# Sliding-window attention and a gated convolution network: casts on two engines, copies for the shifted gate blocks, fillers on TensorE, and a target for each task

## The chip, the cores and the metric

The kernel runs on one core of one Trainium2 chip. The metric is the device time of one execution in microseconds. Five engines share the work: TensorE (PE, with weight loads shown apart as PEld), VectorE (DVE), ScalarE (ACT), GpSimd (POOL) and SyncE (SP), whose queue issues nearly all DMAs.

## The reference, cut to what matters

```python
# q, k, v: 8 batches x 8 heads x 576 rows x 64 columns, float32
scores = q @ k.T / sqrt(64)                 # only |row - column| <= 32 counts
attn = softmax(scores) @ v                  # per head; heads side by side: x is 8 x 576 x 512
h = maximum(x @ w_in, 0)                    # 512 -> 1024
conv = sum over kk of conv_w[kk] * h shifted by kk - 1 along the rows   # 3 taps per channel
out = (h * sigmoid(conv)) @ w_out           # 1024 -> 512, float32
```

## The kernel before

**Attention.** A batch has eight heads, worked on in four pairs. q, k and v come from DRAM in float32 into staging tiles (`qkst`, `vst`) and are cast to bf16 (`qkb`, `ve`). `ve` holds v in blocks of 128 rows with a column of ones; `vo` is the same shifted by 64 rows, made by two copies of 64 partitions. `transposes` turns q and k on PE (18 small products each) and copies them out of PSUM into `qT` and `kT`. `scores` makes nine bands of 128 x 64 for a pair, takes the exponential on ACT (two calls, 640 and 512 elements) and multiplies by a band mask on DVE (`attn<-attn,mask`, 1152 elements). `values` multiplies by v (the ones give the sum), takes the reciprocal and scales into `xn`. `x_turned` turns `xn` on PE and copies it to `xT`.

**The network.** The rows of two batches (1152) are cut into three chunks of 384, so there are twelve chunks, c = 0 to 11; chunk 1 is done in two halves. `first` multiplies by w_in in eight blocks m of 128 channels (four products each) and writes half of the rectified result to `hT`. `gates` does the three taps as 48 small products of 32 x 32 weights per group of four blocks (`hT,diag_w`), takes tanh on ACT (two calls per group) into `tn`, and makes three products on DVE (`gT<-tn,hT` and `gT<-tn,gT`), which give twice h times the sigmoid. The small products put channel block m on partitions turned by 32 times (m mod 4). So for three blocks of four, h has to stand in `gT` in the same turned order: `moves` does that with DMAs from `hT` to `gT` on SP's queue. The w_out rows are loaded turned in the same way. `second` multiplies `gT` by w_out, 128 rows at a time, eight products each, copies the result to `wst` and stores it. PSUM is one tile of eight banks; a task that opens banks gets them when their readers are done. `ws` (`wst`) is also the staging of w_in and w_out.

**What sets the order.** Nothing runs in the order in which it is written. Each step is a task, put in by `Order.add` with the engines it may run on and a modelled time for each, the data it reads and writes, the banks it opens, and a target time t. `Order.run` is a list scheduler that plays all engines forward in modelled time: an engine takes the ready task with the smallest target; a task with a choice of ACT or DVE goes where it ends first. The instructions are emitted in the order found, and each engine keeps that order on the chip. The targets follow from some thirty numbers in `PARAMS`: when a pair of heads or a chunk starts and how far each kind of step lies from that. All casts are tasks of POOL alone. Most instructions are issued through one helper line, line 274, so the profile's rows are told apart by tile and shape.

The functions that the change and the prediction touch are `Order.add`, `Order.run`, `loads`, `load_w_in`, `load_w_out`, `transposes`, `scores`, `values`, `x_turned`, `first`, `moves`, `gates`, `second` and `ffn`.

Of the kernel before, what the change touches and what calls it, by code (L numbers as in the profile page):

```python
# [14 lines left out]
RING = 3100  # L15

# [15 lines left out]
class Order:  # L32
# [3 lines left out]
    def __init__(self):  # L36
        self.tasks, self.writer, self.readers = [], {}, {}

    def add(self, kinds, emit, t, reads=(), writes=(), opens=None, ps=(), after=(), claims=()):


        deps = set(after)
# [10 lines left out]
        task = Task(len(self.tasks), kinds, emit, t, deps, opens, ps)  # L53
        task.soft = soft - deps
        for k in reads:
            self.readers.setdefault(k, []).append(task)
# [8 lines left out]
    def run(self, emit=True):  # L65
        free = {"PE": 0.0, "ACT": 2800.0, "DVE": 6000.0, "POOL": 4400.0, "SP": 800.0}
        mode, channel, backlog = None, 0.0, []
        bank_free = [0.0] * 8
        for x in self.tasks:
# [39 lines left out]
        while pending:  # L109
            best = None  # L110
            for e, xs in ready.items():
# [5 lines left out]
                while pick is None:  # L117
# [28 lines left out]
            if len(x.kinds) > 1:  # L146
                def done(k):
                    return max(free[k], x.ready) + x.kinds[k][1]
                f = min(x.kinds, key=done)
                if f != e:  # L150
                    e, now = f, max(free[f], x.ready)
                    busy, result, more = x.kinds[e]
            if e == "PE":
                if more != mode:
                    busy, result, mode = busy + 90.0, result + 90.0, more
            if e == "SP":
# [8 lines left out]
                result = channel + slack - now  # L165
            free[e] = now + busy
# [28 lines left out]
def kernel(  # L195
# [53 lines left out]
    hT_pp = [sb([128, MB, CH + (4 if i == 1 else 2)], BF16, f"hT{i}") for i in range(3)]  # L249
# [14 lines left out]
    mask = sb([128, 2, S], BF16, "mask")  # L264

# [24 lines left out]
    def pl(n):  # L290
        return 150 + 0.85 * n, 200 + 0.85 * n, None
# [12 lines left out]
    o = Order()  # L304
    nc.scalar.dma_start(conv_w24, moe_conv_w.rearrange("k (m p) -> (k m) p", p=128))
# [32 lines left out]


# [8 lines left out]

    def loads(b):
        i = b % NLD  # L350

        def load_qk(y, j):
# [4 lines left out]
            )  # L357

# [21 lines left out]
        if b < 2:  # L380
            x, dx = (-100.0 if b == 0 else -50.0), 0.1
# [5 lines left out]
        def paced():  # L387
            return before[-2:-1] if b > 1 and len(before) > 1 else []

        for j in range(NPH):  # L390
            for y in range(2):
                t = x + n * dx
                o.add({"SP": dma(256, 110)}, lambda e, y=y, j=j: load_qk(y, j), t,
                      writes=[("st", y, j)], after=paced())
                before.append(o.tasks[-1])
                o.add({"POOL": pl(1152)}, lambda e, y=y, j=j: cast_qk(y, j, e), t,
                      reads=[("st", y, j)], writes=[("b", i, y, j)])
                n += 1
        for c in range(NBLK):
            t = x + n * dx  # L400
            o.add({"SP": dma(1024, 21)}, lambda e, c=c: load_v(c), t, writes=[("vst", c)], after=paced())
            before.append(o.tasks[-1])
            o.add({"POOL": pl(512)}, lambda e, c=c: cast_v(c, e), t,
                  reads=[("vst", c)], writes=[("ve", i, c)])
            n += 1
        for cs in ((0, 2), (2, 4)) if b == 0 else ((0, 4),):
            for half in range(2):
                o.add({"DVE": dve(520 * (cs[1] - cs[0]), 4)},
                      lambda e, cs=cs, half=half: shift(half, cs), x + n * dx,
                      reads=[("ve", i, c + half) for c in range(*cs)],  # L410
                      writes=[("vo", i, c, half) for c in range(*cs)])

    def load_w_in():
        for h in range(2):
# [9 lines left out]
            o.add({"SP": dma(512, 95)}, load, -60.0, writes=[("ws", 4 * h + c) for c in range(4)])  # L424
            for c in range(KC):
                o.add({"POOL": pl(512)}, lambda e, h=h, c=c: cast(e, h, c), -60.0 + h,
                      reads=[("ws", 4 * h + c)], writes=[("w_in", h, c)])

    def load_w_out():
        rows = moe_w_out.rearrange("(h c p) f -> p h c f", c=4, p=128)  # L430
        for c in range(4):
            def load(e, c=c):
                for lo, at, n in turn(c):
# [5 lines left out]
            o.add({"SP": dma(256, 95, len(turn(c)))}, load, -40.0,  # L439
                  writes=[("ws", 4 * h + c) for h in range(2)])  # L440
            for h in range(2):
                o.add({"POOL": pl(512)}, lambda e, h=h, c=c: copy(e, w_out_sb[:, 4 * h + c, :], ws[:, 4 * h + c, :]),
# [18 lines left out]
    def conv_weights():  # L461
        ps = Banks(1)
        o.add({"PE": pe(200.0, "f32")},
              lambda e: tensor.matmul(bank(ps, 0)[:, 0:3 * MB], conv_w24, ident24, start=True, stop=True),
              5.0, opens=ps, writes=[("cw24",)])
        o.add({"DVE": dve(24)}, lambda e: vector.tensor_copy(
            out=conv_w_sb.rearrange("p k m -> p (k m)"), in_=bank(ps, 0)[:, 0:3 * MB]),
            5.0, reads=[("cw24",)], writes=[("cw",)], ps=[ps])
        o.add({"DVE": dve(768)}, lambda e: vector.tensor_tensor(
# [5 lines left out]
    def transposes(g2):  # L475
# [3 lines left out]
        i, n = b % NLD, g2 % NKT  # L479
        for y in range(2):  # L480
# [16 lines left out]
            o.add({"PE": pe(280.0, "rows")}, mm, t + Q["TR"],  # L497
                  reads=[("b", i, y, j)], writes=[("tr", g2, y)], opens=ps,
                  claims=[("T", n, y, h) for h in range(2)])
            for h in range(2):  # L500
                o.add({"ACT": act(576), "DVE": dve(576)},
                      lambda e, ps=ps, h=h, to=to: copy(
                          e, to[:, h, :, :], half(ps, h).rearrange("p (j x) -> p x j", x=64)),
                      t + Q["TC"], reads=[("tr", g2, y)], writes=[("T", n, y, h)], ps=[ps])
# [4 lines left out]
    def scores(g):  # L509
# [3 lines left out]
        for part, ts in enumerate((range(0, 5), range(5, 9))):  # L513
            ps = Banks(2, 2)
            w = 64 * len(ts)

# [10 lines left out]
            o.add({"PE": pe(28.0 * len(ts), "rows")}, mm, t + Q["SC"] * d,  # L527
# [340 lines left out]
```

## Time and profile before

| what | value |
|---|---|
| median of 3 runs (lowest, highest) | 241.9 us (240.6, 242.52) |
| the profiled execution's own time | 243.37 us |
| its span | 241.7 us |
| PE busy | 208.1 us (86%) |
| ACT busy | 164.0 us (68%) |
| DVE busy | 160.1 us (66%) |
| POOL busy | 80.9 us (33%) |
| read from and written to DRAM | 32.52 MB, 9.44 MB |

An engine's busy time counts the stretches in which at least one of its instructions runs. A group's mean is the length of one instruction, which can overlap the next by a little. "L274" is the helper line. A row of the order of time gives start, length, engine, operation, tiles and count, and in brackets how long the engine was idle before it and what ended that wait. A tile's row gives the shortest, median and longest length. PEclk is the share of the full TensorE clock that was granted.

### The profile page before, as it was taken

To read this page: it belongs to the slowest core of one execution; us is meant where nothing else is said; L and a number is where in the kernel's file an instruction comes from. 1 tells how busy PE (TensorE), PEld (TensorE's weight loads), DVE (VectorE), ACT (ScalarE), POOL (GpSimd) and SP (SyncE) were. 2 spreads that over 40 slices of the span, in tenths; PEclk is the share of its full clock that TensorE was granted. 3 is DMA by queue.
4 is the path that set the end of the run, shared out by engine and by line. 5 is a ranking of instruction groups with operands and counts; after the bars stand their busy time and mean duration, and the time that the engine had idled before them with its cause. 6 is when DMAs were issued, how large, how long until landed. Compare 5 with 4: busy or idle time off the path is not lost. (4 is left out here: it accounts for less than half of the span.)

```text
span 241.7 us, 9128 instructions
## 1 busy us (share of the span) xinstructions
PE 208.1 (86%) x3878; PEld 124.3 (51%) x3906; DVE 160.1 (66%) x268; ACT 164.0 (68%) x291; POOL 80.9 (33%) x96
## 2 busy tenths in 40 slices
PE   1536995589998869999999998999999999999993
PEld 0425464365655454565455654655555655555541
DVE  7586166998575899546399779698684595524140
ACT  1650586445698576679977886679778885876751
POOL 5757744536613444662236517321000000000000
PEclk9999999758999997999999999999999999999999
DMA  6999999989698899969489989756132223342534
GB/s 237 292 289 392 248 233 223 275 229 337 168 290 186 217 293 355 328 186 278 98 207 356 264 225 281 161 129 205 37 129 55 79 105 68 123 110 54 177 113 181
DMA packets 67228, 49.62 MB, mean 205 GB/s; under 512 B 46172, under 2 KB 52340, under 8 KB 67188
## 3 DMA queue, kind: packets, MB, share of 16 engines
q1 hardware_dynamic: 67152, 49.03, 71.6%
q8 instruction: 30, 0.49, 0.9%
q14 instruction: 10, 0.08, 0.1%
q10 hardware_dynamic: 36, 0.01, 0.0%
HBM read 32.52 MB, written 9.44 MB: 174 GB/s over the span
## 5 line engine op out<-in xcount | busy, mean ns | idle before, releaser
L274 PE MATMUL pst<-xT,w_in_sb 128*128 128x385 bf16 (+2 forms) x416 | 75.4, 322 | 1.6 <-ACT xT L274 0.6
L274 PE MATMUL pst<-w_out_sb,gT 128*128 128x512 bf16 x260 | 64.3, 384 | 3.2 <-issue 2.2
L274 PEld LDWEIGHTS <-w_in_sb 128*128 128x128 bf16 x416 | 37.6, 100 | 25.8 <-issue 3.4
L274 ACT ACTIVATE hT<-pst 128x385 bf16<-128x385 f32 (+2 forms) x80 | 38.6, 489 | 11.1 <-PE pst L274 10.1
L274 DVE SCALAR_TENSOR_TENSOR gT<-tn,gT 128x384 bf16<-128x384 f32 (+2 forms) x52 | 42.4, 842 | 3.9 <-DMA gT<-hT 3.9
L274 POOL CAST ve<-vst 128x512 bf16<-128x512 f32 x40 | 29.4, 741 | 45.7 <-DMA vst<-in_v_dram 43.5
L274 ACT ACTIVATE attn<-pst 128x640 bf16<-128x640 f32 x64 | 39.4, 667 | 4.9 <-PE pst L274 4.9
L274 PEld LDWEIGHTS <-gT 128*128 128x128 bf16 x288 | 26.6, 99 | 31.0 <-issue 3.3
L274 ACT ACTIVATE tn<-pst 128x768 f32<-128x768 f32 (+1 forms) x52 | 37.4, 768 | 6.5 <-PE pst L274 4.6
L274 ACT COPY wst<-pst 128x512 f32<-128x512 f32 x36 | 21.2, 588 | 29.6 <-PE pst L274 28.1
L274 DVE TENSOR_TENSOR attn<-attn,mask 128x1152 bf16<-128x1152 bf16 x32 | 26.9, 846 | 12.3 <-ACT attn L274 12.1
L274 DVE TENSOR_TENSOR xn<-pst,rec 128x640 bf16<-128x640 f32 x32 | 25.8, 818 | 0.5
L274 DVE SCALAR_TENSOR_TENSOR gT<-tn,hT 128x384 bf16<-128x384 f32 (+1 forms) x26 | 14.7, 564 | 16.5 <-ACT tn L274 16.4
L274 POOL CAST qb<-qst 128x1152 bf16<-128x1152 f32 x16 | 19.9, 1242 | 16.2 <-DMA qst<-in_q_dram 12.5
L274 POOL CAST kb<-kst 128x1152 bf16<-128x1152 f32 x16 | 19.9, 1243 | 16.0 <-DMA kst<-in_k_dram 14.3
L274 PE MATMUL pst<-hT,diag_w 32*32 32x384 bf16 (+1 forms) x1248 | 21.2, 322 | 1.8 <-DVE xn L274 1.0
L274 ACT COPY xT<-pst 128x1024 bf16<-128x1024 bf16 (+1 forms) x16 | 11.8, 781 | 13.9 <-PE pst L274 13.9
L274 PEld LDWEIGHTS <-attn 128*64 128x64 bf16 x640 | 14.1, 119 | 13.6 <-issue 8.6
L274 PE MATMUL pst<-ve,attn 128*64 128x65 bf16 x384 | 17.4, 206 | 3.8 <-DVE attn L274 2.3
L274 PE MATMUL pst<-qT,kT 64*128 64x64 bf16 x576 | 17.5, 197 | 3.1 <-DVE kT L274 0.8
L274 PE MATMUL pst<-vo,attn 128*64 128x65 bf16 x256 | 15.6, 206 | 3.3 <-DVE vo L274 3.3
L274 PEld LDWEIGHTS <-kT 64*128 64x128 bf16 x576 | 12.2, 98 | 12.0 <-issue 9.2
(37 smaller groups left out, 163.4 us busy)
## 6 DMA issues: line engine op xcount, KB each, us to landing
qst<-in_q_dram SPq DMA_DIRECT2D x16, 576.0 KB, 6.4
kst<-in_k_dram SPq DMA_DIRECT2D x16, 576.0 KB, 7.3
out_dram<-wst SPq DMA_DIRECT2D x11, 768.0 KB, 5.8
vst<-in_v_dram SPq DMA_DIRECT2D x24, 256.0 KB, 5.5
vst<-in_v_dram SPq DMA_DIRECT2D x16, 192.0 KB, 5.9
wst<-in_moe_w_in_dram SPq DMA_DIRECT2D x2, 1024.0 KB, 7.9
gT<-hT SPq DMA_DIRECT2D x14, 144.0 KB, 3.6
gT<-hT SPq DMA_DIRECT2D x34, 48.0 KB, 2.1
```

The costliest lines, as they stand in the source:

```text
L274: return lambda *args, **kwargs: fixed(do(*args, **kwargs))
```

## The change

1. **Casts on ACT or POOL.** Every cast of q, k, v, w_in and w_out may now run on either, wherever it is planned to end first.
2. **A port in the plan.** The scheduler has one more resource, `port`. POOL's tasks and DVE's tasks with two inputs in SBUF (and the copies between SBUF tiles) may not overlap in planned time. Nothing on the chip enforces it.
3. **Copies in place of moves.** For all twelve chunks `moves` now issues copies from `hT` to `gT`, 32 or 64 partitions at a time, on DVE or ACT. `hT` gets one leading column. The DMA form remains in the text for c >= `GE`, and there are only twelve chunks.
4. **Fillers.** Where the plan shows PE idle, before 95 us, it gets products of a constant tile, 128 x 512, written to a bank that PE's next task opens and overwrites: 28 of them.
5. **A target for each task.** The list `TIMES` gives a target for every task of a kind, in the order in which they are added, instead of the formula. `PARAMS` changes too.
6. **Batch 0 in halves.** q and k of batch 0 are loaded, cast and turned in two halves of 32 partitions; some k loads go through ACT's queue. Scores, masks and values of batch 0 come in two parts, and the first product of chunk 0 too. w_in's halves are loaded behind the halves of batch 0.
7. **Smaller things.** The table for the exponential is loaded by a small call at the start; the rule that a load waits for the second load before it is off.

The program orders show this count: POOL had all 88 casts; after the change there are 92 (batch 0's are halves), 53 on POOL and 39 on ACT. DVE gets 121 copies and ACT 49 for the moves. SP issues 102 DMAs fewer for the moves.

The core of the diff:

```diff
+        t = next(self.times[name], t) if name in self.times else t
...
+                if pick and pick[1].kinds[e][2] == "port":
+                    pick = (max(pick[0], port), pick[1], pick[2])
...
+            if more == "port":
+                port = now + busy
...
+            if e == "PE" and emit and now < KEEP:
+                since = max(free[e], bank_free[where[0]], 4000.0)
+                self.warm(int((now - since - 300.0) / (260.0 if free[e] > 4000.0 else 430.0)), where[0])
...
-    hT_pp = [sb([128, MB, CH + (4 if i == 1 else 2)], BF16, f"hT{i}") for i in range(3)]
+    hT_pp = [sb([128, MB, CH + (6 if i == 1 else 4)], BF16, f"hT{i}")[:, :, 1:] for i in range(3)]
...
+    def warm(n, i):
+        for _ in range(n):
+            tensor.matmul(pst[:, i, :], warm_sb[:, 0:128], warm_sb, start=True, stop=True)
...
-            return before[-2:-1] if b > 1 and len(before) > 1 else []
+            return before[-2:-1] if b > 1 and len(before) > 1 and not GE else []
...
-                o.add({"POOL": pl(1152)}, lambda e, y=y, j=j: cast_qk(y, j, e), t,
+                o.add("qc", {"POOL": pl(1152), "ACT": act(1152)}, lambda e, y=y, j=j: cast_qk(y, j, e), t,
...
             ms = [4 * qd + s_ for qd in qds]
+            wide = 64 if s_ == 2 else 32
+            for lo in range(0, 128, wide) if c < GE else ():
+                to = (lo + 32 * s_) % 128
+                def shift(e, m=ms[0], lo=lo, to=to, wide=wide):
+                    if len(qds) > 1:
+                        copy(e, gate(m, to, to + wide, 2, 4), taps(m, 1, lo, lo + wide, 2))
+                    else:
+                        copy(e, gate(m, to, to + wide), taps(m, 1, lo, lo + wide))
+                o.add("mc", {"DVE": two(dve(n * len(qds) + 60, 3.4)), "ACT": act(n * len(qds))},
+                      shift, t + Q["MC"], reads=[("h", kind, m, p_) for m in ms for p_ in halves],
...
-            o.add({"DVE": dve(n * count)}, product, late,
+            o.add("pr", {"DVE": two(dve(n * count))}, product, late,
...
+        if c == 0:
+            for m in range(MB):
+                first(c, m, 0, T0 + Q["A0"] + m * 0.5)
```

More of the change, by code (lines that the diff above doesn't have):

```diff
@@ L15 @@
 RING = 3100
+KEEP = 95000.0
+GE = 12
 class Banks:
@@ L53, in add @@
         task = Task(len(self.tasks), kinds, emit, t, deps, opens, ps)
+        if line:
+            soft.add(line[-1])
+        if line is not None:
+            line.append(task)
         task.soft = soft - deps
+        task.tag = (name, index)
         for k in reads:
@@ L357, in load_qk, with load_half, cast_half @@
             )
+        def load_half(y, j, half):
+            for e_ in range(2):
+                src = (q, k)[y][b, 4 * j + 2 * e_:4 * j + 2 * e_ + 2, 32 * RP * half:32 * RP * half + 32 * RP, :]
+                (scalar if y and not half else sync).dma_start(
+                    qkst[y][j][64 * e_:64 * e_ + 64, half, :, :].rearrange("p j d -> p (j d)"),
+                    bass.AP(src.tensor, src.offset, [[RP * D, 32], [S * D, 2], [1, RP * D]]),
+                )
+        def cast_half(y, j, half, e):
+            copy(e, half_of(y, j, half), qkst[y][j][:, half, :, :])
         def cast_qk(y, j, e):
@@ L437, in load @@
                     )
[L439 to L440 removed]
+            o.add("wo", {"SP": dma(256, 95, len(turn(c)))}, load, -90.0,
+                  writes=[("ws", 4 * h + c) for h in range(2)], line=lead)
             for h in range(2):
[L442 removed]
+                o.add("woc", {"POOL": pl(512), "ACT": act(512)}, lambda e, h=h, c=c: copy(e, w_out_sb[:, 4 * h + c, :], ws[:, 4 * h + c, :]),
                       T1 - 2 + h, reads=[("ws", 4 * h + c)], writes=[("w_out", 4 * h + c)])
@@ L479, in transposes @@
         i, n = b % NLD, g2 % NKT
+        if b == 0:
+            for half in range(2):
+                for y in range(2):
+                    transposes_half(g2, y, half, t + Q["B0"] * half)
+            return
         for y in range(2):
@@ L820 @@
             scores(2 * g2 + 1)
-        for i in range(NP):
-            values(b * NP + i)
+        for part in (0, 1) if b == 0 else (None,):
+            for i in range(NP):
+                values(b * NP + i, part)
         for c, n in ((0, 2), (2, 2), (4, 1)):
```

267 lines of the change are left out of this document (183 added, 84 removed), and 114 rows, old and new, of tables (PARAMS, TIMES).

## Prediction

> **What bounds the kernel now.** I read the busy time of each engine by stretches first, cut where a stage of the work ends: 42 is where the last of chunk 0's tanh calls ends, 70 chunk 1's, 122 chunk 4's, 174 chunk 7's.
>
> ```profile
> core 0: us, PE busy (x) PEld busy (x) DVE busy (x) ACT busy (x) POOL busy (x), PEclk, DMA share, GB/s
> 0.00:42.00 42.00, 24.66 (x514) 17.75 (x514) 25.51 (x57) 20.52 (x35) 25.62 (x38) 1.00 1.01 274
> 42.00:70.00 28.00, 23.63 (x528) 15.69 (x530) 23.13 (x39) 16.63 (x34) 14.69 (x15) 0.82 0.87 258
> 70.00:122.00 52.00, 47.44 (x914) 27.85 (x917) 36.21 (x56) 40.68 (x72) 21.40 (x24) 0.97 0.87 240
> 122.00:174.00 52.00, 49.72 (x965) 28.72 (x973) 42.48 (x65) 39.86 (x73) 19.16 (x20) 1.00 0.78 216
> 174.00:221.00 47.00, 46.00 (x801) 26.28 (x805) 27.85 (x48) 36.33 (x66) 0.00 (x0) 1.00 0.30 90
> ```
>
> From 122 on PE is the bound (95.7 of 99 us busy). Before it, PE is short of work: it misses 17.3, 4.4 and 4.6 us in the first three stretches, and DMA is busy 0.87 to 1.01 there. So the start is bound by loads, casts and the chain of small attention steps, the rest by PE. Next, the order of time around the first uses of both weights, and the end:
>
> ```profile
> 25.54 4.12 PE L274 MATMUL pst<-xT,w_in_sb 128*128 128x385 bf16 x16 [0.55 <-ACT xT L274]
> 42.11 3.27 POOL L274 CAST w_out_sb<-wst 128x512 bf16<-128x512 f32 x4 [1.39 <-DMA wst<-in_moe_w_out_dram]
> 54.62 2.37 PE L274 MATMUL pst<-w_out_sb,gT 128*128 128x512 bf16 x7
> ...
> 120.51 1.51 ACT L274 ACTIVATE tn<-pst 128x768 f32<-128x768 f32 x2 [0.15 <-PE pst L274]
> ...
> 231.13 6.85 PE L274 MATMUL pst<-w_out_sb,gT 128*128 128x512 bf16 x31 [0.16 <-issue]
> 238.07 0.59 ACT L274 COPY wst<-pst 128x512 f32<-128x512 f32 x1 [1.20 <-PE pst L274]
> ```
>
> The first product with w_in starts at 25.5, the first with w_out at 54.6, twelve microseconds after the last w_out block landed (42.1). The chip then works through PE's queue until 238.0; the last store adds 3.7 to the span's 241.7. The profiled execution took 243.4, its span 241.7; the median of the three runs is 241.9, so I make the sum on the span and add 0.2.
>
> **The change part by part.** The program order of each engine gives the counts; every stretch below is cut at the same event, chunk 4's last tanh (the 24th on ACT; 122.0 before).
>
> *Copies in place of moves.* All 102 issues of shifted gate blocks leave SP's queue and the DMA; 170 copies come, 121 on DVE, 49 on ACT.
>
> ```profile
> L274 SPq DMA_DIRECT2D gT<-hT x102: 496/627/1922, 34.6 to 230.2; - x102
> ...
> L274 DVE COPY vo<-ve x18: 425/698/1587, 13.8 to 167.2; 64x2080 bf16<-64x2080 bf16 x14, 64x1040 bf16<-64x1040 bf16 x4
> ```
> ```profile
> L274 ACT COPY wst<-pst 128x512 f32<-128x512 f32 x36 | 21.2, 588 | 29.6 <-PE pst L274 28.1 <-issue 1.0 <-POOL ve L274 0.5
> L274 ACT COPY xT<-pst 128x1024 bf16<-128x1024 bf16 x10 | 10.1, 1017 | 13.7 <-PE pst L274 13.7
> L274 ACT COPY qT<-pst 128x576 bf16<-128x576 bf16 x23 | 14.2, 647 | 0.3 <-PE pst L274 0.3
> L274 DVE COPY xT<-pst 128x1024 bf16<-128x1024 bf16 x6 | 4.1, 691 | 7.8 <-PE pst L274 7.7
> L274 DVE COPY kT<-pst 128x576 bf16<-128x576 bf16 x13 | 9.7, 750 | 3.0 <-PE pst L274 2.9
> ```
>
> The nearest DVE row is the vo copy, also bf16 from SBUF to SBUF across partitions: 0.425 us for 1040 elements and 0.70 for 2080 undisturbed, so 0.15 + 0.000264 per element: 0.35 us for 768, 0.25 for 384. The other end is the kT row, one element at a time out of PSUM (0.750 for 576): 0.95 and 0.55. I take the fast end because hT gets a leading column in the same change, which puts the middle tap on an even element as vo's is. ACT: the line through 588 (512) and 1017 (1024) gives 0.80 and 0.48. Up to chunk 4 the cost is 21 x 0.35 + 29 x 0.25 = 14.7 us of DVE and 9 x 0.80 + 11 x 0.48 = 12.5 us of ACT. SP gains 102 x about 0.63 us of issue, in which its loads and stores stood behind it. The later loads also lose their pacing (each waited for the second one before it), so they start once their staging is free; I cost that at nothing, hidden from 122 on by PE's own work, and its failure is the loads rival below.
>
> *Casts.* 39 of 92 now stand on ACT, 53 on POOL (88 before); up to chunk 4 ACT gets: 10 of 1152 elements (1.13 by the line), 22 of 512 (0.59), 3 of 576 (0.65), 26.2 us. Against it, ten copies of xT and wst go from ACT to DVE (-9.0), and half-size pieces of batch 0 and chunk 0 add 5.7. ACT: 12.5 + 26.2 - 9.0 + 5.7 = +35.4 us in whole lengths; DVE: 14.7 + 7.6 of moved xT and wst copies + 10.3 of pieces = +32.6. Lengths overlap in a queue: before, ACT's own instructions up to there add up to 84.4 by such lengths where the first three stretches show 77.8 busy, DVE's 90.7 against 84.9. So after the change ACT has 110.5 us of busy time by that event and DVE 115. If all follow without a gap, less: two tanh calls take 1.51 where the group's mean is 0.819 each, 0.13 less per instruction, which makes ACT's 196 instructions 102 us.
>
> *The start.* Batch 0 comes in halves and chunk 0's first product is cut in two, so half of it no longer waits for the whole batch. ACT begins at 5.4 instead of waiting for the first copies, but has 2 us of gaps until the loads are in. Both engines then carry what PE waits for. So chunk 4's last tanh falls between 5.4 + 102 = 107.4 and 5.4 + 110.5 + 2 = 117.9 without any other waits; I take the middle of 102 and 110.5, with the 2 us: 113.6 instead of 122.0.
>
> *Fillers.* 28 products of 512 columns, 0.22 each by the last PE row above (6.85 / 31): 6.2 us. They lie in gaps that the planned times show, and cost nothing while the next task waits for ACT or DVE longer than they last; if no gap is there, 6.2. What they can bring:
>
> ```profile
> 45.00:55.00 10.00, 7.22 (x173) 5.20 (x168) 9.14 (x17) 3.67 (x6) 3.82 (x4) 0.52 0.88 279
> 55.00:60.00 5.00, 4.89 (x59) 2.81 (x60) 4.76 (x7) 2.72 (x7) 2.92 (x4) 0.94 1.10 329
> 89.00:93.00 4.00, 3.52 (x41) 2.58 (x42) 3.94 (x4) 3.07 (x5) 2.59 (x3) 0.59 1.08 363
> ```
> ```profile
> 46.14 0.26 PE L274 MATMUL pst<-ve,attn 128*64 128x65 bf16 x1 [1.00 <-DVE attn L274]
> 47.83 0.26 PE L274 MATMUL pst<-ve,attn 128*64 128x65 bf16 x1 [0.93 <-DVE attn L274]
> 49.78 1.67 PE L274 MATMUL pst<-ident,xn 128*128 128x128 bf16 x14 [0.85 <-DVE xn L274]
> ```
>
> The clock stood at 0.52 in 45 to 55 and 0.59 in 89 to 93, with PE busy 7.22 and 3.52: at full clock that is 3.4 and 1.4 us less. I count none of it by itself, since both stretches lie ahead of chunk 4, where ACT and DVE now set the pace. The page "TensorE: Matmul & The Clock Gate" of the Trainium skill (section "Why this matters for your kernels") speaks against fillers here: the clock falls only when PE idles for more than about 3 us between bursts. By that page fillers in gaps of 1 us would bring nothing, only their 6.2 us could count, and the sum would be 236; the rows show the half clock with gaps of 0.85 to 1.00, so the measurement differs, and the sum stays as it is.
>
> *After chunk 4.* By that event the new order has 12 w_in products, 36 transposes, 36 scores and 40 value products more behind it:
>
> ```profile
> 222.48 2.13 PE L274 MATMUL pst<-xT,w_in_sb 128*128 128x385 bf16 x12
> 57.26 0.44 PE L274 MATMUL pst<-ident,qb 64*128 64x64 bf16 x18
> 57.53 0.43 PE L274 MATMUL pst<-ident,kb 64*128 64x64 bf16 x18
> 42.03 0.44 PE L274 MATMUL pst<-qT,kT 64*128 64x64 bf16 x18
> 42.39 0.22 PE L274 MATMUL pst<-ve,attn 128*64 128x65 bf16 x1
> ```
>
> That is 12 x 0.17 + 2 x 0.27 + 2 x 0.36 (start to start) + about 0.7 for the values = 4.0 us. PE needed 238.0 - 122.0 = 116.0 from there; it now needs 112.0, if no wait is added. DVE is what comes late next: between chunks 4 and 7 it gets 32 copies (15 x 0.35 + 17 x 0.25 = 9.5 us) on top of 42.5 in 52 us, which just fits.
>
> **Sum:** 113.6 + 112.0 + 3.7 = 229.3, and 0.2 for the median: 229.5, said as 230. Ends: 107.4 and no PE idling after chunk 4 (3.3 us less than before) give 219.8 with the 3.7; 117.9 gives 233.8.
>
> **The rivals.**
> *The copies are slow (slower).* If a copy runs at the kT row's rate, DVE gets 21 x 0.60 + 29 x 0.30 = 21 us more before chunk 4, that event falls at 134.6 and the time is 251 or more (134.6 + 112.0 + 3.7 + 0.2). It decides from 126.0 on (126.0 + 115.9 = 241.9), 12 us more of DVE. For it: the copies change partitions within the tile and the tap view has two levels. Against it: vo changes partitions too.
> *DVE and POOL hold each other up.* The targets keep two-input DVE tasks away from POOL's by planned times only; nothing enforces it.
>
> ```profile
> L274 DVE TENSOR_TENSOR attn<-attn,mask x32: 695/758/1561, 11.4 to 198.7; 128x1152 bf16<-128x1152 bf16 x32
> ...
> L274 DVE TENSOR_TENSOR attn<-attn,mask 128x1152 bf16<-128x1152 bf16 x32 | 26.9, 846 | 12.3 <-ACT attn L274 12.1
> ```
>
> The mask product takes 695 undisturbed and 846 on average: 0.15 us each. Masks, vo copies, gate products and now gate copies are 124 such tasks by chunk 4 instead of 66; at 0.15 each that is 18.6 us instead of 9.9: the event falls at 122.3 and the time is 238. Against it: POOL has 35 casts fewer. The page "SBUF — State Buffer" of the Trainium skill (section "SBUF: two separate sides") says the same as a lock held for a whole instruction; the 1.59 us of the longest vo copy agrees.
> *The fillers stand in PE's way.* Where the planned gaps are not there, 6.2 us: 236. Against it: the gaps of the three rows above were there with nothing in them.
> *The loads set the start all the same.* w_out's last block landed at 42.1, before most moves were issued, so taking them away may free nothing: chunk 4 at 122, 112.0 + 3.7 + 0.2 behind it, 238. Against it: PE then still sat 9 us until 70.
>
> **How the numbers follow.** Forecast (224 to 235) 0.50; fillers (236) 0.05; engines dense enough for 219 to 224, 0.13; loads (about 238) 0.10; DVE against POOL 0.13, counted as 0.10 within 1% (238 lies just outside, and waits behind it add up) and 0.03 slower; slow copies 0.09. About 1% (2.4 us) is what a measurement of this kernel can tell. Faster: 0.50 + 0.05 + 0.13 + 0.10 = 0.78; within 1%: 0.10; slower: 0.03 + 0.09 = 0.12. The range 219 to 243 leaves out the slow copies and the slower part of DVE against POOL, 0.12.
>
> **What would show it.** gT copies of 768 elements near 0.35 us on DVE and 0.8 on ACT; chunk 4's last tanh near 114 with ACT busy over 90% before it; the first w_out product near 42 to 46; clock near 1.0 from 45 to 93; PE's idle after chunk 4 at 4 us or less. A tanh later than 126, or copies near 0.9 us, make it wrong on the slow side; PE idling less than 10 us between 42 and the end makes it wrong on the fast one.

## The result and the profile after

The changed kernel takes 254.3 us (median of four, 252.23 to 256.03) where the kernel before, measured beside it, takes 241.28. The ratio is 1.0507, with a 95% interval of 1.0444 to 1.057: slower by about 5%. Forecast was 230. Ratios here and below leave out executions that ran long beside the others of their kernel (of the changed kernel the profiled one, 256.03 us with a span of 254.3), so they can differ a little from the quotient of two medians.

First the busy time by stretches after the change, cut as the prediction cuts the kernel before, and one stretch more. Columns: stretch and its length, then busy time and instructions of PE, PEld, DVE, ACT and POOL, the granted clock, the DMA share and rate.

```profile
core 0: us, PE busy (x) PEld busy (x) DVE busy (x) ACT busy (x) POOL busy (x), PEclk, DMA share, GB/s
0.00:42.00 42.00, 30.65 (x564) 21.42 (x568) 28.24 (x79) 28.89 (x51) 14.14 (x26) 1.00 1.01 256
42.00:70.00 28.00, 19.83 (x539) 12.57 (x542) 25.89 (x46) 22.90 (x41) 9.92 (x10) 0.88 1.03 285
70.00:122.00 52.00, 41.35 (x804) 25.84 (x804) 46.12 (x84) 41.08 (x78) 15.12 (x16) 0.93 0.71 216
122.00:174.00 52.00, 49.95 (x908) 27.92 (x918) 47.28 (x90) 47.18 (x78) 7.15 (x9) 1.00 0.54 149
174.00:221.00 47.00, 46.48 (x839) 27.91 (x844) 42.64 (x88) 41.95 (x75) 0.64 (x2) 1.00 0.15 52
```

Between 42 and 122 PE is idle for 18.8 us of 80; before the change it was 8.9. DVE fills 72.0 of those 80 us (59.3 before) and ACT 64.0 (57.3 before). From 122 on PE is the bound, as before. So the loss lies ahead of 122, in a stretch where DVE now has few gaps left.

Next the event at which the prediction cut its sum, chunk 4's last tanh (the second row), from the order of time on ACT; and the same stretches cut at that event.

```profile
139.76 0.83 ACT L295 ACTIVATE tn<-pst 128x768 f32<-128x768 f32 x1
140.46 0.51 ACT L295 ACTIVATE hT<-pst 128x385 bf16<-128x385 f32 x1
140.83 0.85 ACT L295 ACTIVATE tn<-pst 128x768 f32<-128x768 f32 x1
```
```profile
5.40:42.00 36.60, 29.07 (x560) 20.79 (x564) 24.48 (x61) 27.40 (x49) 11.93 (x18) 1.00 1.08 272
42.00:141.70 99.70, 80.08 (x1637) 48.52 (x1645) 89.71 (x163) 82.77 (x148) 27.39 (x27) 0.93 0.80 233
5.40:141.70 136.30, 109.15 (x2196) 69.31 (x2209) 114.19 (x224) 110.17 (x196) 39.32 (x45) 0.95 0.88 244
```

The event ends at 141.7: it was forecast at 113.6 and stood at 122.0 before. From there to the end of the span it is 112.6 us; the prediction had 115.7 (112.0 and the store's 3.7). So the whole miss lies before the event, and what follows went a little better than forecast. The last row holds the second surprise: the work was counted rightly. DVE has 114.2 us of busy time up to the event (115 forecast), ACT 110.2 (110.5 forecast). What was missed is the time in which they were not busy: 22.1 us on DVE and 26.1 on ACT.

Then the mask product and the copies, by shape, their mean length in ns the second number behind the bar; and the tile's row for w_out, whose first product the prediction looked for at 42 to 46.

```profile
L295 DVE TENSOR_TENSOR attn<-attn,mask 128x1152 bf16<-128x1152 bf16 x28 | 22.0, 810 | 1.1 <-ACT attn L295 1.0
L295 DVE COPY gT<-hT 32x768 bf16<-32x768 bf16 x42 | 16.3, 388 | 0.7
L295 DVE COPY gT<-hT 32x384 bf16<-32x384 bf16 x56 | 15.7, 283 | 2.4 <-ACT hT L295 1.3
L295 ACT COPY gT<-hT 32x384 bf16<-32x384 bf16 x24 | 12.2, 509 | 0.5
L295 ACT COPY gT<-hT 32x768 bf16<-32x768 bf16 x14 | 11.6, 829 | 0.3
```
```profile
L295 PE MATMUL pst<-w_out_sb,gT x263: 376/379/634, 54.1 to 250.1; 128*128 128x512 bf16 x132
```

The copies are near the fast end (0.35 and 0.25 forecast for DVE, 0.80 and 0.48 for ACT). But the first product with w_out starts at 54.1, where it started at 54.6 before. It did not wait for the loads alone: the last block of w_out landed at 47.6, but its last cast, now one of ACT's, started only at 52.40.

```profile
52.40 0.62 ACT L295 CAST w_out_sb<-wst 128x512 bf16<-128x512 f32 x1
```

The last view is the chain that ended last, as a share of the span, and the same chain between 42 and the event alone:

```profile
PE 55%; DVE 27%; ACT 8%; issue 5%; DMA 3%; POOL 0%; DVEq 0%; ACTq 0%; POOLq 0%
PE pst L295 55%; DVE gT L295 11%; DVE xn L295 5%; DVE attn L295 3%; DMA kst<-in_k_dram 2%; DVE vo L295 2%; ACT hT L295 2%; DVE hT L295 2%; ACT gT L295 2%; DVE xT L295 2%; ACT tn L295 1%; DVE kT L295 1%; DMA qst<-in_q_dram 1%; DVE rec L295 1%; DVE wst L295 1%
```
```profile
by line: PE pst L295 36.8%; DVE gT L295 22.3%; DVE xn L295 7.6%; issue 6.9%; DVE attn L295 5.2%; DVE vo L295 4.6%; DVE xT L295 2.5%; DVE wst L295 2.2%; DVE hT L295 2.0%; DVE kT L295 1.7%; DVE rec L295 1.7%; DVE qT L295 1.3%; ACT wst L295 1.
```

DVE stands on the chain for 27% of the span, some 69 us, and its largest part (11%) is what writes `gT`: the gate products and the copies. Between 42 and the event DVE's parts make up 51% of the chain and PE's 37%.

### The profile page after: what moved, and what is told of

It is laid out like the page before. It is cut to its first block, busy times and chain, and to the rows that moved or that the text cites. A ratio compares the mean times of both kernels' runs of the same rounds, so it can differ in the third digit from the quotient of the medians.

```text
span 254.3 us, 9280 instructions
## 1 busy us (share of the span) xinstructions
PE 216.7 (85%) x4008; PEld 129.7 (51%) x4038; DVE 209.0 (82%) x429; ACT 205.8 (81%) x361; POOL 47.0 (18%) x61
## 4 chain that ended last, share of the span: by engine, by line
PE 55%; DVE 27%; ACT 8%; issue 5%; DMA 3%; POOL 0%; DVEq 0%; ACTq 0%; POOLq 0%
PE pst L295 55%; DVE gT L295 11%; DVE xn L295 5%; DVE attn L295 3%; DMA kst<-in_k_dram 2%; DVE vo L295 2%; ACT hT L295 2%; DVE hT L295 2%; ACT gT L295 2%; DVE xT L295 2%; ACT tn L295 1%; DVE kT L295 1%; DMA qst<-in_q_dram 1%; DVE rec L295 1%; DVE wst L295 1%
## 5 line engine op out<-in xcount | busy, mean ns | idle before, releaser
L295 PE MATMUL pst<-xT,w_in_sb 128*128 128x385 bf16 (+3 forms) x448 | 73.0, 309 | 3.5 <-DVE hT L295 1.2
L295 DVE COPY gT<-hT 32x384 bf16<-32x384 bf16 (+3 forms) x121 | 40.0, 331 | 4.4 <-ACT hT L295 1.7
L295 ACT ACTIVATE attn<-pst 128x640 bf16<-128x640 f32 (+1 forms) x64 | 39.5, 662 | 2.6 <-PE pst L295 2.5
L295 ACT ACTIVATE hT<-pst 128x385 bf16<-128x385 f32 (+3 forms) x80 | 35.3, 476 | 6.2 <-PE pst L295 5.8
L295 ACT COPY gT<-hT 32x384 bf16<-32x384 bf16 (+3 forms) x49 | 31.4, 640 | 1.5 <-DVE hT L295 0.4
L295 DVE TENSOR_TENSOR attn<-attn,mask 128x1152 bf16<-128x1152 bf16 (+2 forms) x36 | 26.4, 752 | 6.8 <-ACT attn L295 6.4
L295 DVE TENSOR_TENSOR xn<-pst,rec 128x640 bf16<-128x640 f32 (+2 forms) x36 | 26.2, 742 | 0.6
L295 POOL CAST ve<-vst 128x512 bf16<-128x512 f32 x25 | 17.3, 709 | 43.0 <-PE pst L295 27.8
L295 DVE TENSOR_SCALAR hT<-pst 128x385 bf16<-128x385 f32 (+3 forms) x32 | 14.7, 468 | 6.2 <-PE pst L295 4.9
L295 PEld LDWEIGHTS <-diag_w 32*32 32x32 bf16 x1248 | 12.6, 88 | 12.6 <-issue 9.5
```

Source lines behind the costliest of these rows:

```text
L295: return lambda *args, **kwargs: fixed(do(*args, **kwargs))
```

## The experiments

Theory D, formed on these views: the copies bring DVE more work than its gaps ahead of 122 hold, and PE waits for DVE. Rival L: POOL's casts lengthen DVE's instructions, and that is now on the path. Others: the fillers, the targets, the later loads, and (R) an order worked out with times that the chip does not keep. Where nothing else is said, an edit is made to the changed kernel and leaves the order of its tasks alone. "Planned end" is where the kernel's own scheduler expects to finish; it is no measurement. It expected 232.0 for the kernel before and 227.5 after the change, against spans of 241.7 and 254.3. Ratios are to the kernel before, measured beside each run.

### No copies

```diff
             def shift(...):
+                return
...
+    for t_ in gT_pp:
+        vector.memset(t_, 0.0)
```

> The changed kernel with its order kept and the 170 copies from hT to gT left out (gT is cleared once at the start, so the gate products of three blocks in four work on zeros). Theory D (DVE is the bound from about 42 us, where the loads let it go, to chunk 4's last tanh): DVE is rid of 21 x 0.39 + 29 x 0.28 = 16 us ahead of that event, so it falls near 126 instead of 141.7 and the time near 238. Theory L (DVE and POOL hold each other up): the copies lost 4.4 us to it, so about 249. Theory O (the order set by the targets leaves engines waiting on each other, however much work they have): within 3 us of 254.

245.54 us (245.33 to 246.13), ratio 1.0189 [1.0136, 1.0243]. The copies are worth 3.2 of the 5.1% lost, and chunk 4's last tanh ends at 132.6, 9.1 earlier. The rows of the two middle stretches:

```profile
42.00:70.00 28.00, 20.57 (x550) 13.38 (x553) 21.97 (x37) 23.13 (x43) 8.21 (x10) 0.88 0.99 272
70.00:122.00 52.00, 46.78 (x860) 28.24 (x865) 41.31 (x69) 38.53 (x72) 15.59 (x16) 0.93 0.84 242
```

DVE falls to 63.3 us of 80, and PE gains 6.2 us there. The time falls between the two theories' figures, so D is part of the cause and not all of it.

### Short casts on POOL

```diff
-            copy(e, ve_pp[i][:, c, :, 0:64], vst[:, c, :, :])
+            w = 2 if e == "POOL" and b > 1 else 64
+            copy(e, ve_pp[i][:, c, :, 0:w], vst[:, c, :, 0:w])
```

(and 16 columns in the same way for q and k)

> The changed kernel with its order kept; POOL's casts of batches 2 to 7 do 16 columns instead of 512 or 1152 (the rest of those tiles keeps the values of batches 0 and 1). Theory L: DVE's instructions are 11.6 us longer in 42 to 122 than their shortest; without POOL in the way most of it goes, and the time is near 243. Theory D alone: DVE's own work stays, about 251. Theory O: 252 to 254.

246.16 us (243.23 to 249.22), ratio 1.0134 [0.9994, 1.0273]. With all copies in place, but POOL busy for 7.9 us instead of 25.0 between 42 and 122, about as much comes back as without the copies (3.7 of the 5.1%, with a wide interval). These are the mask products and copies of that run, to be set beside the 810, 388 and 283 of the changed kernel above:

```profile
L295 DVE TENSOR_TENSOR attn<-attn,mask 128x1152 bf16<-128x1152 bf16 x28 | 20.4, 749 | 1.2 <-ACT attn L295 1.0
L295 DVE COPY gT<-hT 32x768 bf16<-32x768 bf16 x42 | 14.8, 353 | 0.8
L295 DVE COPY gT<-hT 32x384 bf16<-32x384 bf16 x56 | 14.0, 252 | 2.5 <-ACT hT L295 1.4
```

So the copies' own lengths are exactly those forecast, 0.35 and 0.25; 0.03 on each, and 0.06 on each mask, is POOL's doing. POOL itself holds 0% of the chain above, so it is not the casts' own length that was felt. Summed over DVE, each instruction against the 10th percentile of its own shape, the lengthening is about 17 us in the changed kernel and 4 here. It was about 16 before the change, so over the whole run it hardly grew; ahead of chunk 4's last tanh it went from about 11 to 15. What changed more is that the gaps that took it up are gone.

### Neither

Both edits above.

> The changed kernel with its order kept, with both edits of before at once: the copies from hT to gT left out (gT cleared at the start) and POOL's casts of batches 2 to 7 cut to 16 columns. Alone they gained 9 and 8 us. If both are costs of DVE's one queue they add up, less the 4.4 us that the copies lost to POOL: about 241. If each only moves the wait elsewhere: 245, as with one of them.

245.12 us (242.45 to 246.49), ratio 1.0063 [1.0019, 1.0106]. The two causes overlap: 4.4% together, against 3.2 and 3.7 singly (by the intervals, that both together win more than short casts alone is not shown). And with both gone the kernel only stands where the kernel before stands, 0.6% above it.

```profile
42.00:70.00 28.00, 22.88 (x565) 14.52 (x565) 21.46 (x41) 24.32 (x46) 3.64 (x10) 0.88 1.03 285
70.00:122.00 52.00, 47.26 (x923) 28.09 (x923) 39.17 (x69) 38.74 (x71) 3.55 (x15) 0.97 0.85 251
122.00:174.00 52.00, 52.00 (x1005) 29.95 (x1005) 38.40 (x64) 41.64 (x74) 1.75 (x10) 1.00 0.44 124
```

The chain between 42 and chunk 4's last tanh (129.7 here), to be set beside the one above:

```profile
by line: PE pst L295 69.7%; issue 7.3%; ACT tn L295 4.3%; DVE xn L295 3.6%; ACT attn L295 2.6%; ACT qb L295 2.4%; ACT kT L295 2.0%; ACT hT L295 1.7%; DVE wst L295 1.3%; ACT w_out_sb L295 1.2%; DVE xT L295 0.8%; DVE rec L295 0.8%; DVE gT L29
```

PE is idle for 9.9 us between 42 and 122, near the 8.9 of before, and not at all from 122 to 174, and the chain runs through PE's products for 70% instead of 37. In this order nearly all of the excess over before is accounted for; the forecast gain is still missing.

### Smaller loads, and all three

```diff
-        ... bass.AP(src.tensor, src.offset, [[RP * D, 128], [2 * S * D, 2], [1, RP * D]]),
+        ... bass.AP(src.tensor, src.offset, [[RP * D, 128], [2 * S * D, 2], [1, RP * D // (4 if b > 1 else 1)]]),
```

(the same for v)

> The changed kernel with its order kept; the loads of q, k and v of batches 2 to 7 bring a quarter of the bytes (the rest of the staging keeps old values). Theory S (the loads come late, since they stand behind casts in ACT's and POOL's queues and behind each other): the step of 5 us that the tanh calls lose against the plan at about 105 us is gone, 249. Theory D and L (DVE's queue and its quarrel with POOL): within 2 us of 254.

251.03 us (248.22 to 252.23), ratio 1.0292 [1.0195, 1.0389], between the two figures, with the DMA share at 0.44 and 0.25 in the two middle stretches. Some 2% hangs on the later loads.

> The changed kernel, order kept, without the copies (those blocks of gT stay zero), with POOL's casts of batches 2 and later cut to 16 columns, and with a quarter of the bytes in the loads of those batches (part of the attention input is left out). Planned end 227.5. If late loads are what is left over: 232 to 237, at least 6 below the run without the first two. If something else is (short products with gaps, the clock, the start): 240 to 245, as that run.

240.51 us (239.22 to 242.52), ratio 0.9882 [0.9794, 0.9969]. The loads give 1.8% more, but not the 8 us that were looked for: with all three left out, the span of 240.8 is still 13 us behind the planned 227.5. The later loads are not most of what is left.

### The fillers, the targets, the leading column

```diff
-    o.warm = warm
+    o.warm = lambda n, i: None
```

> The changed kernel with its order kept, without the 28 filler products. Theory F (fillers stand in PE's way): up to 6 us faster, 248. Theory D: PE waits for DVE anyway, within 1.5 us of 254. If the fillers hold the clock up: slower by 2 to 5 us.

252.54 us (251.12 to 254.37), ratio 1.0501 [1.0406, 1.0596]: as with the fillers. The stretch from 42 to 70 ran at a clock of 0.82 without them and 0.88 with them, but two other runs that kept the fillers and this order (smaller loads, and the leading column below) show 0.82 too, so that the fillers hold the clock up is not shown. This run also shows what PE does before 42 when no filler is counted:

```profile
0.00:42.00 42.00, 25.98 (x521) 21.47 (x522) 26.52 (x77) 26.86 (x48) 14.60 (x26) 0.96 1.01 258
```

26.0 us, where the kernel before had 24.7, at a clock of 0.96 against 1.00: the new start puts at most 1.3 us more of PE's work ahead of 42.

```diff
-TIMES = {...}
+TIMES = {}
```

> The changed kernel without the list of targets: each target comes from the formula and the new numbers of PARAMS. All the work is the same, the order is not. Theory O (the listed targets make an order that the chip can't follow): faster, near 245. Theory D and L: the same work passes through DVE, so about as slow or slower, 252 to 265.

256.91 us (254.13 to 259.13), ratio 1.0551 [1.0464, 1.0639]: no difference that can be told from the changed kernel's. Its scheduler expects this order to end at 238.4, 10.9 us later than with the list: the targets win that much in the plan and nothing that the chip shows.

```diff
-    hT_pp = [sb([128, MB, CH + (6 if i == 1 else 4)], BF16, f"hT{i}")[:, :, 1:] for i in range(3)]
+    hT_pp = [sb([128, MB, CH + (6 if i == 1 else 4)], BF16, f"hT{i}") for i in range(3)]
```

> The changed kernel with its order kept, hT without its leading column, so that the middle tap starts on an odd element and a copy should take up to 0.95 us for 768 elements and 0.55 for 384. Theory D: DVE gets up to 21 x 0.56 + 29 x 0.27 = 20 us more ahead of chunk 4's last tanh and the time rises by about as much, to 270 or more. Theory O: by less than 6 us. If the copies keep their length, nothing is shown.

254.91 us (252.62 to 255.59), ratio 1.0557 [1.0461, 1.0653]. The copies kept their length: 389 and 287 ns, against 388 and 283. So this run could not serve as a dose of dearer copies, and the prediction's ground for the fast end (the leading column) did not matter.

### Copies alone in the kernel before, and casts alone

The copies of the change put into the kernel before; its scheduler orders everything anew.

> The kernel before with one part of the change alone: copies from hT to gT on DVE or ACT in place of the moves. Theory D: in the old order DVE has room (16, 5 and 16 us in the first three stretches), so little is lost: 240 to 246. Theory L: POOL still does all 88 casts there, each copy loses 0.1 us and more, and the old mask and gate products more: 248 or more.

262.29 us (260.62 to 263.25), ratio 1.0804 [1.0743, 1.0865]. Here POOL still has all casts, and each makes the other worse:

```profile
42.00:70.00 28.00, 18.11 (x403) 10.69 (x403) 25.66 (x34) 17.36 (x33) 15.53 (x14) 0.76 0.73 227
70.00:122.00 52.00, 43.37 (x808) 25.92 (x806) 46.82 (x78) 37.66 (x66) 23.93 (x25) 0.84 0.88 239
```
```profile
L274 DVE TENSOR_TENSOR attn<-attn,mask 128x1152 bf16<-128x1152 bf16 x32 | 29.8, 935 | 4.5 <-ACT attn L274 4.1
L274 DVE COPY gT<-hT 32x768 bf16<-32x768 bf16 x34 | 14.5, 426 | 0.9
```

PE idles for 18.5 us of the 80, as in the changed kernel, and the mask takes 935 instead of 846. In an order with the old parameters the copies by themselves are a loss, and a larger one than the whole change; those parameters were never fitted to copies.

```diff
-            o.add({"POOL": pl(512)}, lambda e, c=c: cast_v(c, e), t,
+            o.add({"POOL": pl(512), "ACT": act(512)}, lambda e, c=c: cast_v(c, e), t,
```

(the same for q, k and both weights, in the kernel before)

> The kernel before with one part of the change alone: all casts may go to ACT or POOL. Theory L (POOL's casts lengthen DVE's instructions, 16.5 us in all in the profile of before): 2 to 5 faster than before, 237 to 240, with DVE's lengthening below 10. Rival C (ACT cannot carry them): 244 or more, with ACT's busy time up by 15 to 20.

242.98 us (242.93 to 246.35), ratio 1.0132 [0.9989, 1.0274]. POOL's busy time falls from 80.9 to 51.6, ACT's rises from 164.0 to 180.6, and nothing is won; the time lies between the two figures. ACT took over what POOL was rid of, so the run does not tell what relieving POOL alone is worth there.

### What the moves had cost

```diff
             def move(e, m=ms[0], s_=s_):
+                return
...
+    for t_ in gT_pp:
+        vector.memset(t_, 0.0)
```

In the kernel before, order kept.

> The kernel before without its shifted gate blocks (those blocks of gT stay zero, so part of the gate is left out); all else and the order kept. If the moves held something up before the change: 236 to 239. If they were hidden behind PE's work: 240 to 242.5, and then copies in their place had nothing to win.

252.22 us, ratio 1.0401 [1.0315, 1.0487], and that number must not be taken as it stands. I had put the three clearings of `gT` ahead of everything else on DVE, and they delayed the start. The first tanh in the kernel before:

```profile
31.76 1.51 ACT L274 ACTIVATE tn<-pst 128x768 f32<-128x768 f32 x2
```

and the first tanh and the last copy of the result in this run (the latter started at 238.07 before):

```profile
40.77 1.51 ACT L274 ACTIVATE tn<-pst 128x768 f32<-128x768 f32 x2
...
247.79 0.59 ACT L274 COPY wst<-pst 128x512 f32<-128x512 f32 x1 [1.20 <-PE pst L274]
```

The start is 9.0 us late and the end 9.7. Without its moves the kernel made up nothing of a late start, so I read the moves as hidden; the run doesn't show it cleanly. The page of before agrees. This is the group of the gate products that read moved blocks, with what DVE waited for ahead of them behind the last bar:

```profile
L274 DVE SCALAR_TENSOR_TENSOR gT<-tn,gT 128x384 bf16<-128x384 f32 (+2 forms) x52 | 42.4, 842 | 3.9 <-DMA gT<-hT 3.9
```

All 102 moves together held DVE up for 3.9 us. (In the runs without copies above, the clearings stand later, and the first scaling into `xn` is 1.6 us late; the first tanh is not late.)

### Moves in the new order

Each copy issued as a DMA at its own place, order kept:

```diff
-                        copy(e, gate(m, to, to + wide), taps(m, 1, lo, lo + wide))
+                        sync.dma_start(gate(m, to, to + wide), taps(m, 1, lo, lo + wide))
```

> The changed kernel, its order kept task by task, but each of the 170 copies is issued as a DMA move from SP's queue at its place. If it is the copies' work on DVE and ACT that costs: 246 to 250, near the run without copies, plus the moves' way through the queue. If it is the order, which lets the gate product follow 0.3 us behind a copy, that a move cannot keep: 252 to 260.

315.88 us (315.2 to 317.45), ratio 1.3021 [1.2903, 1.3139], far above both figures. 170 issues go into SP's queue at places that were chosen for engines' own instructions, and loads stand behind them. The waits of the products that write `gT`, from the tile's view:

```profile
L295 SPq DMA_DIRECT2D gT<-hT x170: 512/596/2668, 34.6 to 301.6; - x170
...
  DMA gT<-hT: 63.3, 12
```

63.3 us of waiting in 12 places. This says that an order made for copies cannot carry moves; it says nothing on which of the two is dearer in an order of its own. So the moves were put back with a new order:

```diff
-GE = 12
+GE = 0
```

(the loads still not paced)

> The changed kernel with its shifted gate blocks moved by DMA again, as before the change, and all else of the change kept (casts on ACT or POOL, halves of batch 0, the rule for two-input DVE tasks, fillers, targets, no pacing of the later loads). The planner orders everything anew. Theory D (the copies are the main cost, because DVE and ACT are what the stretch from 42 to 110 waits for): 240 to 245, DVE's busy time back near 165 to 170 and chunk 4's last tanh at 128 or earlier. Rival C (the casts on ACT and the new start cost as much): 248 or more. If the rest of the change is worth what its plan says, 236.

254.34 us (253.28 to 259.14), ratio 1.0555 [1.0422, 1.0688]. Theory D expected 240 to 245 and an event by 128; DVE's busy time did fall to 163.7, but the event came at 135.3. This speaks against the copies as the only cause. But the run is weak evidence: the changed kernel's `PARAMS` count a move at no length beyond its transfer (`MV` is 0, where the kernel before has 2000 ns), so this order relied on moves landing too early. The same holds for the next two.

> As the run with DMA moves, and the loads of batches 2 and later wait for the second load before, as they did before the change. If the loads without pacing hold up the moves in the queue: 2 to 5 faster than the run without pacing. If SP's queue is no limit: the same within 1%.

260.27 us (257.55 to 261.66), where the run without pacing has 253.28 to 254.42 in three of its four executions: the old rule for the loads, in this order, makes it slower, which neither expectation had.

```diff
-            for lo in range(0, 128, wide) if c < GE else ():
+            for lo in range(0, 128, wide) if c >= 6 else ():
```

> The changed kernel with copies for chunks 6 to 11 only and DMA moves for chunks 0 to 5. Theory D (a copy costs only where DVE is full, up to about 110; later PE sets the pace and DVE has room): within 1% of the run with DMA moves throughout, though DVE does about 20 us more. If a copy costs wherever it stands: 5 or more above that run, half of what the copies cost in the changed kernel.

262.08 us (256.22 to 263.93). Its executions lie too far apart to be set against the run with moves throughout: the lowest is 1.9 above that run's 254.34, the others 6.7 to 9.6. By theory D late copies should cost nothing. Orders made with parameters never fitted to them cannot tell this apart.

### An order made with dearer instructions

In the changed kernel the plan gives DVE 176.9 us of work and ACT 182.7; the trace has 209.0 and 205.8. Before, it was 140.4 and 147.6 against 160.1 and 164.0. That is 0.06 to 0.08 us too little per instruction, before and after (32.1 us over DVE's 429 instructions, 19.7 over its 268 before), so the shortfall was larger in the kernel with more instructions. It is no pure price per instruction: about 5 us of either DVE figure are the clearings and small copies at the start, which the plan does not hold, and POOL's lengthening is in both. The change also made the plan bolder: it counts a whole mask product at 680 ns where the kernel before counts 850, and the chip took 810.

```diff
+SLOW = {"DVE": 85.0, "ACT": 75.0, "POOL": 100.0}
...
+        kinds = {e: (k[0] + SLOW[e], k[1] + SLOW[e], k[2]) if e in SLOW else k for e, k in kinds.items()}
...
-PARAMS = {...}
+PARAMS = {...}          # fitted to the earliest planned end under these times
```

> The changed kernel with its order worked out from dearer instructions (each DVE task 85 ns more, ACT 75, POOL 100, which makes the planned busy times of DVE and ACT those of the trace, 209 and 206), the targets dropped and the parameters fitted anew. Planned end 242.3. Theory R (the order was out of step with the chip): 244 to 248, at least 6 below the changed kernel, with a planned-to-measured slip of 6 or less. Theory W (the work on DVE and ACT itself is too much, whatever the order): 250 or more.

248.87 us (247.19 to 249.44), ratio 1.0243 [1.0167, 1.0319]. Half of the loss is gone with all copies and casts in place; the span is 247.7 for a planned end of 242.3, 5.4 apart instead of 26.8. The time lies between the two theories' figures, so R is part of it: the changed kernel's order packed DVE as if its instructions were shorter. Dearer costs and newly fitted parameters came together in this run, and which of the two helped was not separated. And work that was planned at about its real length still ends 2.4% behind the kernel before.

> The same dearer costs and new parameters, with the shifted blocks moved by DMA (planned 2 us each, as in the kernel before) in place of copies. Planned end 234.1. If the copies are the part of the change that costs: 236 to 242, at least 6 below the run with copies. If the rest of the change (casts on ACT, the new start) costs as much: within 3 of the run with copies.

249.48 us (248.1 to 250.95), ratio 1.0292 [1.0217, 1.0368]: within 1 us of the run with copies. In orders fitted for them, copies and moves come out alike, and the rest of the change (casts on ACT, the new start, fillers, no pacing) keeps the kernel some 2.9% behind. Its span of 248.4 is 14.3 behind its plan, though, so this order too is out of step with the chip. Which part of the rest does it was not taken further.

> The kernel before with nothing but its order worked out from the dearer costs, with parameters fitted to them. Planned end 231.0, where the same costs and its old parameters give 242.4. If the chip follows such a plan: 233 to 238, faster than both kernels. If the planner's costs do not matter: 240 to 244.

242.77 us (239.37 to 246.85, ten executions), ratio 1.0008 [0.9954, 1.0063]. Planned end 231.0 instead of 242.4, and the chip shows no gain: the span of 240.7 is 9.7 behind the plan, as it was with the old costs. No version tried here that does the whole computation beats the kernel before.

## Why the prediction was wrong, step by step

**The step that failed** is "The start": "ACT begins at 5.4 instead of waiting for the first copies, but has 2 us of gaps until the loads are in. Both engines then carry what PE waits for." It turned busy time into elapsed time by adding 2 us, and took ACT's, at 102 to 110.5, though DVE's stood at 115. (The 102 does not come out of the numbers beside it: 84.4 + 35.4 less 196 x 0.13 is 94. With DVE's 115 in its place the same sum gives 122.4 for the event and 238 for the time.) The trace puts in its place, from the rows cut at the event:

- By 42 DVE had done 24.5 us of the 114.2 since 5.4, and had been idle for 12.1. That the loads set the pace there, as before, is read from the DMA share (1.01 in both kernels); no run cut those loads.
- DVE then had 89.7 us left. Even without a gap the event could not come before 42 + 89.7 = 131.7, and with 112.6 behind it that is 244.3: slower than before. It had 10.0 us of gaps, which makes 141.7.
- The prediction's own first fence showed DVE idle for 30% and ACT for 36% of the time up to 122, while they waited for loads and for one another. The change filled part of those waits (from 0 to the event DVE was idle for 37.2 us before and 23.8 after); the sum had them gone.

**The missing gain.** PE gave a floor that was never worked out. By 122 PE had been busy for 95.7 us before the change, the new order puts 4.0 more ahead of the event by the prediction's count, and some 25 are done by 42; so 42 + 75 = 117 is the earliest at the clock granted before, without one idle microsecond and without fillers. At full clock it would be 112 (the prediction works out 3.4 and 1.4 us less for the two slow stretches). So 113.6 asked for a PE with hardly a gap and at nearly full clock, where it had idled for 8.9 us of the 80. In the run with neither cause the event ends at 129.7: PE is busy for 77.8 us of the 87.7 since 42, fillers included, and idles for the other 9.9.

**Copies in place of moves.** Counts, lengths and sums of work were right. What was wrong is what they replaced: a transfer that DVE waited 3.9 us for in all. "SP gains 102 x about 0.63 us of issue" was a gain on a queue that the prediction showed nothing to wait for. The slow-copies rival named the outcome's size (251 or more), but by chance: the copies were not slow and DVE's work was as forecast. The event passed that rival's 126.0 because of the time in which DVE was not busy.

**DVE and POOL.** This rival came true in its price (8.7 us there; short casts brought back 3.7%, about 9) and only in part in its mechanism: ahead of the event the lengthening grew from about 11 us to 15, not from 9.9 to 18.6. The page "SBUF — State Buffer" of the Trainium skill (section "SBUF: two separate sides") has the one engine locked out for the other's whole instruction. The run with short casts agrees in that masks take 749 instead of 810 ns without POOL in the way; whether by such a lock, these means do not show.

**Loads set the start.** Its sign came, the first w_out product at 54.1 against 54.6, but not by its mechanism alone: the last w_out cast started on ACT 4.8 us after the last block had landed. The rival put the event at 122 and so missed what DVE had behind the start.

**Fillers** cost nothing and brought nothing that the time shows. The clock near 1.0 from 45 to 93 did not come about either (0.88 from 42 to 70). **After chunk 4** the sum nearly held: 112.6 against 115.7, though DVE got busier there as well.

**What stays open.** In the changed kernel's order, copies and POOL's casts hold 4.4 of the 5.1%. In an order made with dearer instructions half of the loss goes without touching either, so the three are not separate sums; I take each to loosen the same full stretch. Why the new start and the casts on ACT, with moves and an order of their own, stay 2.9% behind was not settled.

## What to carry to other kernels

Busy time is no elapsed time: before summing an engine's work up to an event, find when its inputs let it begin, and work out the floor of every engine from there, the one that is not thought to be the bound too. Moving hidden transfers onto an engine costs time once that engine's gaps are used up (here about 9 us at chunk 4's last tanh, for 14.7 us of DVE copies ahead of it), and the idle column beside the transfer's reader (here 3.9 us) says about what there is to win. A plan that counts instructions too short makes a change that adds instructions look better than it is: the planned gain was 4.5 us, and the gap between plan and chip went from 9.7 to 26.8. Dearer costs alone do not make a plan true: with them the gap was 5.4, 14.3 and 9.7.

## What the runs showed of the hardware

- DVE copies of 32 partitions to other partitions took 0.353 us for 768 bf16 elements and 0.252 for 384 when POOL did little. With POOL at work they took 0.388 and 0.283, and without the leading column in the source 0.389 and 0.287.
- With copies added and POOL doing all casts, the 128 x 1152 mask product went from 846 to 935 ns on average; in the changed kernel it went from 810 to 749 when most of POOL's casts were cut short.
- With batch 0 loaded in halves, the first 42 us moved 256 GB/s in the changed kernel (241 to 266 in the runs that kept the halves), against 274 before (265 to 275 with whole loads), at a DMA share of 0.96 to 1.03 in all of them. w_out's loads are issued at 34.45 instead of 30.07. The halves were not undone by themselves, so that they are the cause was not shown.
